# Idle products in the tensor engine's first waits, and q of units 6 to 10 transposed on the tensor engine

## The chip, the cores and the metric

The kernel runs on one core of a Trainium2 chip. The metric is the device time of one execution in microseconds. The engines are called as the profile calls them: PE multiplies matrices (PEld is its weight load), DVE and POOL work on vectors, ACT copies and activates, SP issues most transfers.

## The reference

A retention block and a feed-forward block without nonlinearity, in fp32:

```python
# q, k, v: (8, 8, 576, 64)   gamma[h] = 1 - 2**(-5 - h)
scores = 1/sqrt(64) * (q @ k.T)
ret = (scores * where(i >= j, gamma[h]**(i - j), 0)) @ v
x = ret.transpose(0, 2, 1, 3).reshape(4608, 512)
out = ((x @ w1) * (x @ w2) @ w3) @ w_out       # w1, w2: 512x1024, w3: 1024x1024, w_out: 1024x512
```

The four weight matrices arrive as 64-bit floats and are converted to fp32 on the chip.

## The kernel before

**Attention.** The eight batches go in four pairs, and the 576 positions in five pieces, one of 64 (the short one) and four of 128. A piece of a pair is a unit: unit g has pair g // 5 and piece g % 5, and there are 20. For a unit, `load` brings q, k and v with positions on the partitions (512 KB each, 256 KB for a short unit), in runs of 64 floats. `scale` multiplies q and v by the decays, mostly on POOL, in the first pair partly on ACT. `front` turns k and q so that the head's dimension lies on the partitions: PE transposes eight blocks of a tensor into two `tp` tiles of PSUM, and ACT copies these to `kT` and `qT`. `score` multiplies them and DVE masks (`pm`, line 246). `state` (line 265) sums k by v over the pieces, and ACT copies the sum to `sb`. `pv` (lines 293 and 300) makes the output, and ACT copies it to the feed-forward block's input `xT`.

**Loads by blocks.** `load_blocks` brings q or k in blocks of 32x32 instead, each in its transposed place: 16 transfers of 32 KB for a full unit, 8 for a short one, in runs of 32 floats. `scale_blocks` scales q in two halves on POOL, and `front_blocks` turns all blocks in place with one DVE transpose for each tensor (line 200), so that PE and ACT have no part in it. The units from 11 on have both q and k by blocks. In the kernel before, units 6 to 10 have q by blocks and k by `load` and `front`.

**Feed-forward.** `up` computes the products with w1 and w2 for 384 tokens and a quarter of the columns in seven products of halves (Strassen's scheme; lines 497, 502 and 523). Each of the seven is four fp32 matmuls of 128x128 by 192 columns. The first, p1, has no sums as operands; the second, S2 by T2, needs sums of weights (`strassen_weights`, `wS`, line 160) and of tokens (`strassen_tokens`, `T`, line 471). `down` does the rest with w3 @ w_out (line 603), which is multiplied out once (`w3_mm`, line 452).

**The order.** All engines work strictly in the order in which the program issues to them; the order is written out by hand at the end of the function. In the first 60 us loads of units 0 to 4, weight blocks (`load_block`, tiles `raw`) and their conversion on DVE and ACT (lines 370 to 402) alternate with the first units' attention and the first steps of `up`. SP issues the loads in that order. Weights are converted from five `raw` buffers. `convert(n)` puts n pieces of a conversion between other work on DVE.

After the weights, a loop runs over units 5 to 19. In its turn g it loads unit g + 2, turns unit g + 1 (`front`), does `down` or `up` steps from a list (`work`), then pv of g, state and scores of g + 1, and the scaling of q of unit g + 2.

**Memory in PSUM.** One pool, `acc`, of seven buffers in rotation, holds `tp`, `sc`, `xps`, `up`, `po` and the small `gps`. An eighth holds the state.

Of the kernel before, what the change touches and what calls it, by code (L numbers as in the profile page):

```python
# [8 lines left out]
F32 = mybir.dt.float32  # L9
# [31 lines left out]
def kernel(  # L41
# [13 lines left out]
    nc = tc.nc  # L55
# [6 lines left out]
    P = 128  # L62
# [6 lines left out]
    NC = (S + P - 1) // P  # L69
# [30 lines left out]
    acc = ctx.enter_context(tc.tile_pool(name="acc", bufs=7, space=PSUM))  # L100
# [33 lines left out]
    nc.scalar.dma_start(dq, decay_q)  # L134
    nc.scalar.dma_start(gk[:short, 0, :], decay_k[:short, :])
    nc.scalar.dma_start(gk[:, 1:, :], decay_k[short:, :].rearrange("(c p) h -> p c h", p=P))
    gps = acc.tile([P, NC, H], F32, tag="acc", name="gps")
    for c in range(NC):
        nc.tensor.transpose(gps[:sizes[c], c, :], dq[:, starts[c]:starts[c] + sizes[c]], ident[:H, :H])
    for c in (0, slice(1, NC)):  # L140
        n = short if c == 0 else P
        nc.vector.tensor_copy(gq[:n, c, :], gps[:n, c, :])

# [46 lines left out]
                out=part, in0=part, in1=gqs[:, :, n0:n0 + n].unsqueeze(3).to_broadcast([P, NP, n, BL]),  # L192
                op=ALU.mult)

    def front_blocks(g, names="kq"):
        c = g % NC
        n = sizes[c] // BL
        for nm in names:
            dst = pools["fr"].tile([P, 2, NP, P], F32, tag=nm + "T", name=nm + "T", bufs=1 if nm == "k" else 2)
            nc.vector.transpose(  # L200
                dst[:, :, :, :sizes[c]].rearrange("p b m (n x) -> p (b m) n x", x=BL),
                live["bl_" + nm, g][:, :, :n, :])
            live[nm + "T", g] = dst
# [13 lines left out]
    def front(g, names="kq"):  # L217
        c = g % NC
        sz = sizes[c]
        for nm in names:  # L220
            src = live[nm, g]
            dst = pools["fr"].tile([P, 2, NP, P], F32, tag=nm + "T", name=nm + "T",
                                   bufs=1 if nm == "k" and g >= NC else 2)
            for b in range(2):
                tp = acc.tile([P, NP, P], F32, tag="acc", name="tp")
                for p in range(NP):
                    h = b * H + 2 * p
                    nc.tensor.transpose(tp[:, p, :sz],  # L228
                                        src[:sz, h:h + 2, :].rearrange("p a d -> p (a d)"),
                                        ident[:sz, :sz])  # L230
                nc.scalar.copy(dst[:, b, :, :sz], tp[:, :, :sz])
            live[nm + "T", g] = dst
# [39 lines left out]
    def pv(g):  # L272
        i, c = divmod(g, NC)
        sz = sizes[c]
        live["x", g] = True
        qT, vs, pm = live["qT", g], live["v", g], live["pm", g]

        parts = []
        for n in range(NB):
            lo, hi = max(starts[c], n * TB), min(starts[c] + sz, (n + 1) * TB)  # L280
            if lo < hi:
                m = i * NB + n
                if ("xT", m) not in live:
                    live["xT", m] = xps[m % 4 == 3].tile([P, NP, 2, TB], F32, tag="xT", name="xT")
                parts.append((live["xT", m], lo - n * TB, lo - starts[c], hi - lo))

        banks = [acc.tile([P, 2, 2, P], F32, tag="acc", name="xps") for r in range(2)]
        order = [(b, n) for b in range(2) for n in range(2)]
        if c > 0:
            for m, (b, n) in enumerate(order):  # L290
                for r, j in ((0, 0), (0, 1), (1, 0), (1, 1)):
                    p = 2 * r + n
                    nc.tensor.matmul(banks[r][heads[j ^ r], b, n, :sz], live["sb", g][heads[j], b, p, :],  # L293
                                     qT[heads[j], b, p, :sz], start=(m == 0), stop=False,
                                     skip_group_check=True)
        for m, (b, n) in enumerate(order):
            for r in range(2):
                for half in range(2):
                    p, j = 2 * r + n, half ^ r
                    nc.tensor.matmul(banks[r][heads[half], b, n, :sz], vs[:sz, b * H + 2 * p + j, :],  # L300
                                     pm[:sz, b, j, p, :sz], start=(c == 0 and m == 0), stop=True,
                                     skip_group_check=True)
        for x, to, fr, n in parts:
            for r in range(2):
                nc.scalar.copy(  # L305
                    x[:, 2 * r:2 * r + 2, :, to:to + n].rearrange("p n b s -> p b n s"),
                    banks[r][:, :, :, fr:fr + n])
# [169 lines left out]
        minus(B[0][1], B[1][1], B[0][1])  # L477
        minus(T[2], B[1][0], T[1])

    def up(i, n, fp, conv=0, tail=True):  # L480
        m = every.index((i, n))
        while ("S", fp) not in live:
            assert go_on() is None
        if ("B", i, n) not in live:
            strassen_tokens(i, n)
        if fp == 0:
            live["ab", i, n] = (pools["ab3"] if m == 2 else ffn).tile([P, 2 * KF, TB], F32, tag="ab", name="ab")
        ab = live["ab", i, n]

        def product(ps, a, b):  # L490
            a, b = A(fp, a), live["B", i, n][b]
            new = ps is None
            if new:
                ps = acc.tile([P, 2, TB], F32, tag="acc", name="up")
            for w in range(2):
                for r in range(2):
                    nc.tensor.matmul(ps[:, w, :], a[:, w, r, :], b[:, r, :], start=(new and w == r == 0),  # L497
                                     stop=(w == r == 1), skip_group_check=True)
            return ps

        def plus(ps, to, sb):
            nc.vector.tensor_add(c[:, to], ps, c[:, sb])  # L502
            convert(conv)
            if aside:
                aside.pop(0)()


        c = ffn.tile([P, 4, 2, TB], F32, tag="c", name="c", bufs=1)
        p1 = product(None, "A11", "B11")
        nc.scalar.copy(c[:, 0], p1)  # L510
        plus(product(None, "S2", "T2"), 1, 0)
        plus(product(None, "S3", "T3"), 2, 1)
        p5 = product(None, "S1", "T1")
        plus(p5, 3, 2)
        plus(product(None, "A22", "-T4"), 2, 2)
        product(p1, "A12", "B21")
        nc.scalar.copy(c[:, 0], p1)  # L517
        product(p5, "S4", "B22")
        plus(p5, 1, 1)

        if fp == NQ - 1 and m + 1 < len(every) and has_x(*every[m + 1]) and ("B", *every[m + 1]) not in live:
            strassen_tokens(*every[m + 1])
        nc.vector.tensor_mul(ab[:, 4 * fp:4 * fp + 4, :], c[:, :, 0, :], c[:, :, 1, :])  # L523
        if tail:
            convert(conv)
# [130 lines left out]
    load(1, "v")  # L656
    load_block()
    scale(0, "q")
    front(0)
    convert(3)  # L660
    score(0)
    scale(0, "v")
# [6 lines left out]
    convert_up_to(2)  # L669
    load_block()  # L670
    scale(1, "q")
    front(1)
    convert(3)
    scale(1, "v")
    score(1)
# [4 lines left out]
    first_sums = strassen_weights(0)  # L680
    next(first_sums)
    pv(1)
    load(3, "kqv")
    load_block()
    strassen_tokens(0, 0, nc.vector)
# [1 line left out]
        pass  # L687
    scale(2, "q", True)
    aside.append(lambda: scale(2, "v", True))
    up(0, 0, 0, conv=2, tail=False)  # L690
    front(2)
    convert(1)
    scale(3, "q")
# [63 lines left out]
    carry(2, 2)  # L757
    weights_part.close()
    open_attention(ctx)
    load(NC, "kqv")  # L760
    load(NC + 1, "kv")
    load_blocks(NC + 1, "q")
    keep_stores.clear()
    store()
    todo = [(down, (0, 0), (0, 1)), (down, (1, 0), (1, 1)), (down, (0, 2), (1, 2))]
# [33 lines left out]
    front(NC)  # L799
    state(NC)  # L800
    score(NC)
    scale_blocks(NC + 1)
    in_blocks = [u > 2 * NC for u in range(G)] + [False] * 2
    for g in range(NC, G):
        c = g % NC
        n = -(-len(todo) // (NC - c))
        if g + 2 < G and not in_blocks[g + 2]:
            load(g + 2, "k")
            load_blocks(g + 2, "q")
        if g + 1 < G:  # L810
            scale(g + 1, "v")
            if not in_blocks[g + 1]:
                front(g + 1, "k")
                front_blocks(g + 1, "q")
        half = (n + 1) // 2
        if in_blocks[g + 1]:
            scale_blocks(g + 1)
            work(1)
            front_blocks(g + 1)
            half = max(half - 1, 0)  # L820
        if in_blocks[g + 2]:
            load_blocks(g + 2, "q")
            load_blocks(g + 2, "k")
        work(half)
        pv(g)

        if g + 2 < G:
            queue = nc.scalar if in_blocks[g + 2] else nc.sync
            load(g + 2, "v", queue)
            if in_blocks[g + 2] and (g + 2) % NC != NC - 1:  # L830
                load(g + 2, "k", queue)
        if g + 1 < G:
            state(g + 1)
            score(g + 1)
        if g + 2 < G and not in_blocks[g + 2]:
            scale_blocks(g + 2)
        if g == NC + 1:
            strassen_tokens(1, 0)
            todo.extend((up, 1, 0, fp) for fp in range(2))
        work(n // 2)  # L840
        if c == NC - 1:
            add_pair(g // NC)
# [44 lines left out]
```

## Time and profile before

| | |
|---|---|
| median of 3 runs | 864.8 us (864.07 to 865.4) |
| profiled execution | 864.07 us |
| its span, first to last instruction | 862.4 us |
| busy: PE, PEld | 840.2 us (97%), 764.8 us (89%) |
| busy: DVE, ACT, POOL | 473.8 us (55%), 181.6 us (21%), 115.3 us (13%) |
| chain that ended last: PE, DVE, DMA | 85%, 7%, 4% |
| transfers | 63.21 MB, mean 73 GB/s; some 200 GB/s up to 70 us |

An engine's share is an average over stages with different limits. A group's idle time is that of the engine ahead of its instructions; its releaser is inferred from semaphore events. A matmul in fp32 is two records in the trace.

### The profile page before, as it was taken

Reading aid. Unit: us, or ns where it says so; the run is one execution under the profiler, and the core shown is the slowest. Engines: PE = TensorE matmul, PEld = TensorE weight load, DVE = VectorE, ACT = ScalarE, POOL = GpSimd, SP = SyncE. Lnnn points to the kernel's source line nnn. Section 1 sums busy time; section 2 is a strip of 40 time slices with the busy share of each in tenths; the row PEclk is TensorE's granted clock in tenths of the full one; section 3 lists DMA queues with packets and bytes.
Section 4 is the critical chain, followed back from the end, with each engine's and each line's share of the span. In section 5 each row is a group of like instructions: output and inputs, shape, how many; then the busy total and the mean of one; then the engine's idle time right before and its main releaser. Section 6 shows DMA issues by size and latency. Waiting matters only on the chain.

```text
span 862.4 us, 15290 instructions
## 1 busy us (share of the span) xinstructions
PE 840.2 (97%) x6269; PEld 764.8 (89%) x6269; DVE 473.8 (55%) x794; ACT 181.6 (21%) x364; POOL 115.3 (13%) x96
## 2 busy tenths in 40 slices
PE   5899999999999999999999999999999999999998
PEld 5789999644888999999999999999999999999996
DVE  4889998986655344543544453535543434335343
ACT  3666333343121211101111101101101100001000
POOL 3000020001313223203023030230300101000000
PEclk9999999999999999999999999999999999999999
DMA  9994453444346534515142426061300000000001
GB/s 191 218 215 126 99 98 99 122 135 75 48 86 140 110 53 80 87 36 112 32 86 33 77 50 102 22 120 24 52 25 26 2 25 1 25 25 1 25 1 49
DMA packets 204918, 63.21 MB, mean 73 GB/s; under 512 B 186920, under 2 KB 195112, under 8 KB 204848
## 3 DMA queue, kind: packets, MB, share of 16 engines
q1 hardware_dynamic: 172208, 54.07, 30.3%
q10 hardware_dynamic: 32640, 8.16, 5.2%
q8 instruction: 49, 0.80, 0.4%
q14 instruction: 21, 0.17, 0.1%
HBM read 52.76 MB, written 9.44 MB: 72 GB/s over the span
## 4 chain that ended last, share of the span: by engine, by line
PE 85%; DVE 7%; DMA 4%; issue 2%; ACT 1%; SPq 1%; POOL 0%; DVEq 0%; ACTq 0%; POOLq 0%
PE up L497 46%; PE po L603 24%; PE ps L452 4%; PE sc L243 4%; PE xps L300 3%; PE xps L293 2%; PE st L265 1%; DVE c L502 1%; DMA ld_q<-in_q_dram 1%; PE tp L228 1%; DMA raw<-in_moe_w_dram 1%; DVE e L391 1%; DMA ld_k<-in_k_dram 1%; DVE w L402 1%; SPq L725 0%
## 5 line engine op out<-in xcount | busy, mean ns | idle before, releaser
L502 DVE TENSOR_TENSOR c<-up,c 128x384 f32<-128x384 f32 x240 | 133.2, 555 | 183.8 <-PE up L497 179.0
L497 PE MATMUL up<-xT,wA 128*128 128x192 f32 x1152 | 212.1, 327 | 0.7 <-ACT xT L305 0.7
L497 PEld LDWEIGHTS up<-xT,wA 128*128 128x128 f32 x1152 | 190.7, 190 | 3.5 <-ACT xT L305 1.0
L497 PE MATMUL up<-T,wS 128*128 128x192 f32 x768 | 140.6, 326 | 2.4 <-DVE T L471 2.1
L497 PEld LDWEIGHTS up<-T,wS 128*128 128x128 f32 x768 | 127.3, 190 | 2.9 <-issue 2.9
L603 PE MATMUL po<-w3o,ab 128*128 128x256 f32 x456 | 104.3, 380 | 0.3 <-ACT ot L625 0.3
L603 PEld LDWEIGHTS po<-w3o,ab 128*128 128x128 f32 x456 | 85.8, 190 | 12.5 <-ACT ot L625 0.7
L607 DVE TENSOR_TENSOR ot<-po,ot 128x256 f32<-128x256 f32 x90 | 38.2, 424 | 75.0 <-PE po L603 72.2
L497 PE MATMUL up<-xT,wS 128*128 128x192 f32 x384 | 70.6, 327 | 0.6 <-DVE c L502 0.5
L517 ACT COPY c<-up 128x384 f32<-128x384 f32 x48 | 22.9, 477 | 226.2 <-PE up L497 222.0
L246 DVE TENSOR_TENSOR pm<-sc,mask 128x512 f32<-128x512 f32 (+1 forms) x80 | 45.5, 629 | 45.3 <-PE sc L243 45.2
L497 PE MATMUL up<-T,wA 128*128 128x192 f32 x384 | 70.2, 326 | 0.0
L603 PE MATMUL po<-wB,forms 128*128 128x256 f32 x288 | 65.2, 379 | 0.4 <-DVE forms L573 0.4
L497 PEld LDWEIGHTS up<-xT,wS 128*128 128x128 f32 x384 | 63.6, 190 | 1.5 <-DVE c L502 1.5
L497 PEld LDWEIGHTS up<-T,wA 128*128 128x128 f32 x384 | 63.7, 190 | 0.0
L603 PEld LDWEIGHTS po<-wB,forms 128*128 128x128 f32 x288 | 54.6, 190 | 8.2 <-PE po L603 0.8
L214 POOL TENSOR_TENSOR ld_v<-ld_v,gk 128x1024 f32<-128x1024 f32 (+1 forms) x17 | 33.0, 1942 | 199.9 <-DMA ld_v<-in_v_dram 149.8
L452 PE MATMUL ps<-wo,w3T 128*128 128x512 f32 x128 | 56.1, 596 | 2.9 <-DVE w3T L406 2.9
L452 PEld LDWEIGHTS ps<-wo,w3T 128*128 128x128 f32 x128 | 23.8, 190 | 34.5 <-issue 30.6
L471 POOL TENSOR_TENSOR T<-xT,T 128x384 f32<-128x384 f32 x20 | 20.9, 1044 | 216.1 <-PE up L497 214.5
L523 DVE TENSOR_TENSOR ab<-c 128x768 f32<-128x768 f32 x48 | 47.3, 986 | 3.8
L510 ACT COPY c<-up 128x384 f32<-128x384 f32 x48 | 22.8, 476 | 117.8 <-PE up L497 69.1
(73 smaller groups left out, 796.2 us busy)
## 6 DMA issues: line engine op xcount, KB each, us to landing
raw<-in_moe_w_dram SPq DMA_DIRECT2D x64, 128.0 KB, 3.0
bl_q<-in_q_dram SPq DMA_DIRECT2D x208, 32.0 KB, 2.1
out_dram<-ot SPq DMA_DIRECT2D x24, 256.0 KB, 2.0
bl_k<-in_k_dram SPq DMA_DIRECT2D x136, 32.0 KB, 2.2
raw<-in_moe_w_dram SPq DMA_DIRECT2D x8, 512.0 KB, 7.7
raw<-in_moe_w_dram SPq DMA_DIRECT2D x16, 256.0 KB, 7.5
ld_k<-in_k_dram SPq DMA_DIRECT2D x8, 512.0 KB, 6.9
ld_v<-in_v_dram SPq DMA_DIRECT2D x8, 512.0 KB, 7.0
```

What stands on the lines that cost most here:

```text
L214: nc.gpsimd.tensor_tensor(out=t, in0=t, in1=gam[:sz, c].unsqueeze(1).unsqueeze(3).to_broadcast([sz, 2, H, D]), op=ALU.mult)
L243: nc.tensor.matmul(sc[j][:sz, p, :sz], kT[hs, b, p, :sz], qT[hs, b, p, :sz], start=True, stop=True)
L246: nc.vector.tensor_mul(pm[:sz, b, j, :, :sz], sc[j][:sz, :, :sz], mask[:sz, :sz].unsqueeze(1).to_broadcast([sz, NP, sz]))
L300: nc.tensor.matmul(banks[r][heads[half], b, n, :sz], vs[:sz, b * H + 2 * p + j, :], pm[:sz, b, j, p, :sz], start=(c == 0 and m == 0), stop ...
L452: nc.tensor.matmul(ps, live["w3T", ft][:, g, :], live["wo"][:, g, :], start=(g == 0), stop=(g == KF - 1))
L497: nc.tensor.matmul(ps[:, w, :], a[:, w, r, :], b[:, r, :], start=(new and w == r == 0), stop=(w == r == 1), skip_group_check=True)
L502: nc.vector.tensor_add(c[:, to], ps, c[:, sb])
L510: nc.scalar.copy(c[:, 0], p1)
L517: nc.scalar.copy(c[:, 0], p1)
L523: nc.vector.tensor_mul(ab[:, 4 * fp:4 * fp + 4, :], c[:, :, 0, :], c[:, :, 1, :])
L603: nc.tensor.matmul(ps[nm], a[A][:, f, :], live["W"][B][:, f, :], start=(f == 0 and not on), stop=(f == NP - 1), skip_group_check=True)
L607: nc.vector.tensor_add(ot[:, to[0], to[1]], ps[nm], ot[:, sb[0], sb[1]])
```

## The change

The new kernel issues products of the 128x128 identity by itself into an `acc` tile that nobody reads: ten before the transposes of the decays (`gps`), four between k and q of unit 0, six between k and q of unit 1, four behind pv of unit 1, and eight in the first `up`, behind p1. For units 6 to 10, q comes by `load`, is scaled by `scale` and turned by `front` on PE and ACT; `load_blocks`, `scale_blocks` and `front_blocks` remain for units 11 to 19.

```diff
+    warm = acc.tile([P, P], F32, tag="acc", name="idle")
+    for _ in range(10):
+        nc.tensor.matmul(warm, ident, ident, start=True, stop=True)
     gps = acc.tile([P, NC, H], F32, tag="acc", name="gps")
...
+    def keep_busy(n):
+        t = acc.tile([P, P], F32, tag="acc", name="idle")
+        for _ in range(n):
+            nc.tensor.matmul(t, ident, ident, start=True, stop=True)
...
-    def up(i, n, fp, conv=0, tail=True):
+    def up(i, n, fp, conv=0, tail=True, busy=0):
...
         nc.scalar.copy(c[:, 0], p1)
+        if busy:
+            keep_busy(busy)
         plus(product(None, "S2", "T2"), 1, 0)
...
-    front(0)
+    front(0, "k")
+    keep_busy(4)
+    front(0, "q")
...
-    front(1)
+    front(1, "k")
+    keep_busy(6)
+    front(1, "q")
...
     pv(1)
+    keep_busy(4)
     load(3, "kqv")
...
-    up(0, 0, 0, conv=2, tail=False)
+    up(0, 0, 0, conv=2, tail=False, busy=8)
...
-    load(NC, "kqv")
-    load(NC + 1, "kv")
-    load_blocks(NC + 1, "q")
+    for g in (NC, NC + 1):
+        load(g, "kqv")
...
-    scale_blocks(NC + 1)
+    scale(NC + 1, "q")
...
-            load(g + 2, "k")
-            load_blocks(g + 2, "q")
+            load(g + 2, "kq")
...
-                front(g + 1, "k")
-                front_blocks(g + 1, "q")
+                front(g + 1)
...
-            scale_blocks(g + 2)
+            scale(g + 2, "q")
```

More of the change, by code (lines that the diff above doesn't have):

```diff
@@ L193, in scale_blocks, with front_blocks @@
                 op=ALU.mult)
-    def front_blocks(g, names="kq"):
+    def front_blocks(g):
         c = g % NC
         n = sizes[c] // BL
-        for nm in names:
+        for nm in "kq":
             dst = pools["fr"].tile([P, 2, NP, P], F32, tag=nm + "T", name=nm + "T", bufs=1 if nm == "k" else 2)
```

## The prediction

> **What bounds the kernel now.** I read the page first, then the windows by stage, then what PE waited for, then PE's timeline, and last the DMA queue and the chain that ended last. The page:
>
> ```profile
> PE 840.2 (97%) x6269; PEld 764.8 (89%) x6269; DVE 473.8 (55%) x794; ACT 181.6 (21%) x364; POOL 115.3 (13%) x96
> ```
>
> PE is busy for 840.2 of 862.4 us. The windows say where the missing 22 us are not (length, then busy time of PE, PEld, DVE, ACT and POOL, then granted clock, DMA share, GB/s):
>
> ```profile
> 57.60:110.00 52.40, 52.40 (x436) 50.95 (x437) 49.62 (x92) 25.04 (x53) 0.00 (x0) 1.00 0.51 119
> 232.00:328.00 96.00, 95.60 (x1011) 86.64 (x1010) 44.72 (x74) 19.09 (x42) 20.19 (x17) 1.00 0.45 91
> ```
>
> Between 57.6 and 110 us PE has no idle time at all, and in the 96 us in which units 5 to 10 are prepared it has 0.40 us. There an instruction added to PE moves the end by its full length, and one taken from DVE (44.72 of 96) moves nothing. What PE waited for in the first 75 us (total, times, longest):
>
> ```profile
> PE gps L139 <- DMA dq<-decay_q_dram: 6.2, 1, 6.2
> PE tp L228 <- POOL ld_q L214: 3.0, 3, 1.7
> PE up L497 <- DVE T L471: 2.1, 1, 2.1
> PE tp L228 <- DMA ld_k<-in_k_dram: 1.2, 1, 1.2
> ```
>
> With the smaller ones these are 14.0 us, all before 57.55. The first 58 us are thus the only place where the products that are read by nobody can win or lose. PE's timeline (start, length, operation, idle time before it and its releaser):
>
> ```profile
> 16.00 1.97 PE L228 MATMUL tp<-ident,ld_k 128*128 128x128 f32 x8
> 19.63 1.97 PE L228 MATMUL tp<-ident,ld_q 128*128 128x128 f32 x8 [1.67 <-POOL ld_q L214]
> 24.67 1.15 PE L265 MATMUL st<-ld_v,ld_k 128*64 128x64 f32 x32 [0.50 <-POOL ld_v L214]
> 33.15 1.54 PE L497 MATMUL up<-T,wS 128*128 128x192 f32 x8 [2.08 <-DVE T L471]
> 41.26 1.04 PE L228 MATMUL tp<-ident,ld_k 128*128 128x128 f32 x8
> 42.13 1.04 PE L228 MATMUL tp<-ident,ld_q 128*128 128x128 f32 x8
> 44.42 1.06 PE L228 MATMUL tp<-ident,ld_k 128*128 128x128 f32 x8 [1.25 <-DMA ld_k<-in_k_dram]
> 48.81 1.09 PE L228 MATMUL tp<-ident,ld_q 128*128 128x128 f32 x8 [0.26 <-POOL ld_q L214]
> 57.55 1.54 PE L497 MATMUL up<-T,wS 128*128 128x192 f32 x8 [0.30 <-DVE wS L160]
> ```
>
> Two things are to be seen. The same eight transposes take 1.97 us at 16 and 19.6 us and 1.04 us at 41 us: PE runs at half speed early on, though the clock column of the windows reads 1.00 there. And PE comes late to nothing after the first step: it stands still for 1.25 us at 44.42, 0.26 at 48.81 and 0.30 at 57.55, waiting for a load, for a load that POOL scales, and for a weight. Whether those three can come earlier is told by the DMA queue over the first 75 us (packets, MB, share of 16 engines)
>
> ```profile
> q1 hardware_dynamic: 31040, 14.68, 98.9%
> ```
>
> and by the chain that ended last (start, length):
>
> ```profile
> 7.27 9.96 DMA ld_q<-in_q_dram
> ...
> 43.88 9.16 DMA raw<-in_moe_w_dram
> ...
> 53.14 0.43 DVE e L370
> ```
>
> The queue is full (98.9%) until about 71 us. SP's timeline shows each issue following the one before it, with long ones (ld_q from 34.43 for 7.05 us) where the queue has no room. Unit 3's q lands at 46.70 and POOL scales it from 46.86 to 48.76; the raw block issued at 43.88 lands at 53.04, and the seven DVE operations that need it or stand behind it end at 57.41, just before PE's 57.55.
>
> **The change, part by part.** First, the idle products. An fp32 product shows as two records (one `product` of four matmuls is x8). A record of 128 columns takes 0.109 us at full speed: 0.87 us for eight from the start at 41.26 to that at 42.13. In the early rows it takes 1.97/1.04 = 1.9 times that, 0.21. The 10 before `gps` are 20 records, 4.3 us at the slow rate; `ident` is done at 1.37 us, so they end near 5.7, before `gps` at 6.25, which waits for a load in any case. The 4 between k and q of unit 0 are 0.87 us (1.7 slow) against a wait of 1.11. The 6 in unit 1 are 1.31 us (2.6 slow) against 1.67. The 4 behind pv(1) are 0.87 against 0.74, so p1 starts 0.13 late. The 8 behind p1 are 1.74 against 2.08.
>
> What they win: at full speed the rows before 24 us shrink. Beside like rows later on, unit 0's k and q give 0.4 each, its scores 0.9, state 0.9, pv 0.8, unit 1's k and q 0.9 each, its scores 0.6: 5.8 us. But unit 1's q starts when POOL has scaled it (17.36 to 19.58, after the landing at 17.23), so all before that turns into a longer wait at 19.63. The 1.5 us from q and scores of unit 1 turn into a longer wait at 24.67, where `st` needs v, landed at 22.64 and scaled by 24.61. PE then does st, pv and xT as before. DVE gets its scores up to 1.5 us earlier, so T is ready near 31.6 instead of 33.1, but PE is in its fillers to about 33.0 (29.6 + 1.57 + 1.74). The first step starts 0.1 to 0.2 us earlier, and the wait for ld_k at 44.42 takes that back.
>
> What they cost, if the clock stays low and all fillers run slow: q of unit 1 about 1.3 us late, the first step 0.9 to 1.2 late, and the waits at 44.42 and 48.81 have 1.51 to give. From both sides the sum at 57.55 is 0; as bounds I keep -0.3 (the wait there gone) and +0.5 (an overrun somewhat above my 1.2). Each `idle` takes one of seven `acc` buffers; in order of allocation none meets one still being read (the nearest: the second k tile of unit 2 takes p1's, copied by ACT at 40.16, written at 41.7).
>
> A page of the Trainium skill would have this part worth more: "TensorE: Matmul & The Clock Gate", Part 1 and the closing table, says that the array starts at half clock and that some 3.4 us of sustained work release it, so that PE should be kept busy through waits. The halved rows agree with that; yet its advice as a gain would put all 5.8 us into the total, and the landings at 17.23, 22.64, 44.28 and 46.70 let none of it through. By the page's rule alone the sum would be near 863.
>
> Second, q of units 6 to 10 as one plain load each. Gone: 72 block issues on SP (four times 16, once 8; 16 of them took 10 us of SP's time), five transposes on DVE (four of 1.23 us, a shorter one) and ten half-tile scalings on POOL. Added: five loads, five whole-tile scalings on POOL (1.9 to 2.6 us by its rows of L214), ten copies on ACT (0.58 each, ACT busy 19.09 of 96) and forty transposes on PE. Only PE's count. They stand directly behind k's, as at 41.26, so a full unit's q adds 0.87 us, four of them 3.48. Unit 10 is the short one:
>
> ```profile
> 239.79 0.71 PE L228 MATMUL tp<-ident,ld_k 64*128 64x64 f32 x8
> 240.34 0.66 PE L228 MATMUL tp<-ident,ld_q 64*128 64x64 f32 x8
> ```
>
> From start to start 0.55. The sum is 3.48 + 0.55 = +4.03 us. From below 3.85 (107 and 53 ns a record, back to back); from above 4.65, if each eight costs the 1.02 that k's take in the chain by themselves.
>
> The part adds a wait: q's transposes need POOL's scaling, and behind them on PE stands everything else. Before, only DVE waited for it. Let the loads start when SP got to the first block, and give them a plain load's 7 us. Unit 6: landed by about 220, scaled by 223, needed at 243.9. Unit 7: issued at 242.6, scaled by 253, needed at 261. Unit 8: issued at 261.6, scaled by 271, needed at 280. Unit 9: 278.1, 288, 299. Unit 10: 299.0, 307, 314. The smallest margin is 7 us, so this wait costs nothing; without that cover each microsecond of lateness would be one on the end. The two more `acc` tiles per unit meet score tiles that DVE has read (the scores' pm starts at 259.39, the last tile of q would be written near 261.6): 0, at most 0.3 a unit. Nothing later gives the 4 us back: from 330 us to the end PE waits 0.5 us in all, and behind its own products.
>
> The profiled execution took 864.07 us, 1.7 beside its span of 862.4. It becomes 864.07 + 0 + 4.03 = 868.1; the median of the runs is 0.7 above it (864.8), so 868.8.
>
> **The rivals.** Not slower: the first step's earlier start pulls the transfers with it. The place is SP between 27 and 47 us, where raw blocks reuse buffers that DVE has converted; the waits view puts 1.7 us of the issue at 43.88 down to a DVE conversion. If DVE's order and not the queue's room set it, the raw block and ld_q of unit 3 could land earlier by as much as PE gains, at most the 5.8 us: 868.8 - 5.8 = 863.0. It decides from 4.0 us of gain on. Against it: the block that it overwrites was converted at 30.41, 13 us before, and the 0.1 to 0.2 us of head start is all there is to pull.
>
> Slower than forecast: PE waits at the new transposes, for POOL or for an `acc` buffer, by 0.5 us in each of five units: 871.3. Against it stand the margins above.
>
> Slower at the start: the fillers overrun by more than the 1.51 us of slack, say by 1 us: 869.8. That needs the clock to stay low after 24 us, where the profile has it high.
>
> If the unread products were dropped from the program, the time would be the forecast's, since I price them at 0.
>
> **How the numbers follow.** The forecast has 0.83, with 867.6 to 869.9 as its own range (864.07 + 3.85 - 0.3, and 864.8 + 4.65 + 0.5). The waits at the transposes have 0.07, the overrun 0.05, the transfers pulled forward 0.05. A difference of 0.2%, 1.7 us, is about what a measurement of this kernel can tell from none (its three runs lie 1.3 apart). The range goes to 867.5 and 870.3: below little more than that, above for part of the two slower cases. Faster: 0.03, from the pulled transfers at full size; same: 0.04, from these at partial size and from scatter; slower: 0.93.
>
> **What would show it.** Each eight transposes of unit 1 take about 1.05; PE's waits before 19.63 and 24.67 grow; the wait before unit 3's k stays at 44.4, and the second `up` starts its second product near 57.55 as before. From 239.8 on, five rows tp<-ident,ld_q follow those of k with no wait, and each unit's pv comes later by 0.87 more than the last, to 4.0 at 328 us; L200 has five instructions fewer for qT. The forecast is wrong if 57.55 moves by more than half a microsecond, or if a wait for POOL stands before a tp of units 6 to 10.

## The result and the profile after

The changed kernel takes 869.82 us in the median of six runs (868.95 to 870.43), the kernel before beside it 865.12 (864.07 to 865.51): a ratio of 1.0055, with a 95% interval of 1.0042 to 1.0068. That is 4.7 us more; 4.0 were forecast. The profiled execution has a span of 867.7 us, 5.3 more than before.

The page's first part, and the same two stretches of the windows:

```profile
PE 849.2 (98%) x6373; PEld 774.4 (89%) x6373; DVE 468.4 (54%) x789; ACT 186.0 (21%) x374; POOL 113.7 (13%) x91
```

```profile
57.60:110.00 52.40, 52.40 (x439) 51.18 (x438) 49.64 (x92) 25.41 (x53) 0.00 (x0) 1.00 0.53 118
232.00:328.00 96.00, 96.00 (x933) 87.52 (x935) 37.33 (x65) 22.50 (x50) 19.13 (x12) 1.00 0.43 88
```

PE is still without idle time in both, and does its old work later in the second; DVE gave up 7.4 us of the 96, for which nobody waited. PE's waits in the whole span, the longest ones:

```profile
PE ps L461 <- DVE w3T L415: 2.9, 3, 1.3
PE tp L237 <- DMA ld_k<-in_k_dram: 2.2, 2, 1.6
PE tp L237 <- POOL ld_q L223: 2.2, 3, 1.6
PE st L274 <- POOL ld_v L223: 1.8, 2, 1.1
PE po L614 <- DVE ab L580: 1.7, 1, 1.7
```

The first was there before. The second to fourth are the waits of the first 50 us, in new places. The last is new. It stands in the first `down`, for an operand that DVE makes: `ab` is the product of the two `up` results, `forms` are sums of it. PE's timeline shows the places (start, length, operation, idle time and releaser):

```profile
14.96 1.91 PE L237 MATMUL tp<-ident,ld_k 128*128 128x128 f32 x8 [0.59 <-DMA ld_k<-in_k_dram]
16.66 2.35 PE L151 MATMUL idle<-ident 128*128 128x128 f32 x12
20.57 1.10 PE L237 MATMUL tp<-ident,ld_q 128*128 128x128 f32 x8 [1.56 <-POOL ld_q L223]
...
32.94 1.54 PE L506 MATMUL up<-T,wS 128*128 128x192 f32 x8
...
44.59 1.06 PE L237 MATMUL tp<-ident,ld_k 128*128 128x128 f32 x8 [1.63 <-DMA ld_k<-in_k_dram]
48.91 1.09 PE L237 MATMUL tp<-ident,ld_q 128*128 128x128 f32 x8 [0.18 <-POOL ld_q L223]
57.35 1.46 PE L506 MATMUL up<-T,wS 128*128 128x192 f32 x8
```

The first step's second product starts at 32.94 instead of 33.15, unit 3's k waits 1.63 us for its load instead of 1.25, and the second step's second product is 0.20 us ahead of before. Further on, first in the kernel before:

```profile
226.82 5.50 PE L603 MATMUL po<-w3o,ab 128*128 128x256 f32 x24
232.72 3.69 PE L603 MATMUL po<-wB,forms 128*128 128x256 f32 x16 [0.40 <-DVE forms L573]
...
313.63 1.57 PE L497 MATMUL up<-xT,wA 128*128 128x192 f32 x8
```

and then in the kernel after:

```profile
226.54 1.89 PE L614 MATMUL po<-w3o,ab 128*128 128x256 f32 x8
230.18 3.72 PE L614 MATMUL po<-w3o,ab 128*128 128x256 f32 x16 [1.74 <-DVE ab L580]
233.73 3.62 PE L614 MATMUL po<-wB,forms 128*128 128x256 f32 x16
...
262.01 1.09 PE L237 MATMUL tp<-ident,ld_k 128*128 128x128 f32 x8
262.94 1.04 PE L237 MATMUL tp<-ident,ld_q 128*128 128x128 f32 x8
263.81 5.34 PE L614 MATMUL po<-w3o,ab 128*128 128x256 f32 x24
...
317.99 0.66 PE L237 MATMUL tp<-ident,ld_q 64*128 64x64 f32 x8
318.57 1.57 PE L506 MATMUL up<-xT,wA 128*128 128x192 f32 x8
```

The first down starts 0.28 us ahead of before (226.54 against 226.82), then stands for 1.74. From there each full unit's q takes 0.87 us (262.94 to 263.81) without a wait. Against before, PE is 1.01 us late at the forms' product (233.73 against 232.72) and 4.94 at the step behind unit 10's transposes (318.57 against 313.63), so the five units cost 3.93; the remaining 0.4 of the 5.3 come in small pieces later.

### The profile page after: what moved, and what is told of

Same layout as the page of the kernel before. It is cut to its first block, busy times and chain, and to the rows that moved or that the text cites. A ratio compares the mean times of both kernels' runs of the same rounds, so it can differ in the third digit from the quotient of the medians.

```text
span 867.7 us, 15391 instructions
## 1 busy us (share of the span) xinstructions
PE 849.2 (98%) x6373; PEld 774.4 (89%) x6373; DVE 468.4 (54%) x789; ACT 186.0 (21%) x374; POOL 113.7 (13%) x91
## 4 chain that ended last, share of the span: by engine, by line
PE 84%; DVE 6%; issue 2%; ACT 1%; DMA 1%; SPq 0%; DVEq 0%; ACTq 0%
PE up L506 44%; PE po L614 24%; PE ps L461 4%; PE sc L252 4%; PE xps L309 3%; PE xps L302 2%; DVE c L511 2%; PE tp L237 1%; PE st L274 1%; DVE e L400 1%; DVE w L411 1%; DVE m L386 0%; DVE w3T L415 0%; DMA raw<-in_moe_w_out_dram 0%; ACT e L389 0%
```

## The experiments

All times are medians; each ratio is against runs of the kernel before on the same chip, whose median lay between 864.02 and 864.43 us. My first theory after the comparison was that three parts add up: idle products, transposes, and a collision of POOL with DVE near 222 us.

**Each part alone.** First only the idle products on the kernel before:

```diff
+    for _ in range(10):
+        nc.tensor.matmul(warm, ident, ident, start=True, stop=True)
     gps = acc.tile([P, NC, H], F32, tag="acc", name="gps")
...
-    front(0)
+    front(0, "k")
+    keep_busy(4)
+    front(0, "q")
...
-    front(1)
+    front(1, "k")
+    keep_busy(6)
+    front(1, "q")
...
     pv(1)
+    keep_busy(4)
...
-    up(0, 0, 0, conv=2, tail=False)
+    up(0, 0, 0, conv=2, tail=False, busy=8)
```

> The kernel before with the idle products alone. Theory (the three parts add: idle products, q's transposes, and a collision of POOL and DVE near 222 us): 0.5 us less than before, 864.6 against 865.1, since the second product of the second up starts near 57.35 instead of 57.55 and PE is 0.5 us ahead at 67 us; the wait before the forms near 230 us stays at 0.4. Rival (the idle products cost, by their overrun or by shifting what runs against what later): 0.5 to 1.4 us more than before, with a wait of over 1 us near 230 us.

862.5 us against 864.4, ratio 0.9979 (0.9970 to 0.9989): a gain of 1.9 us, where the theory had 0.5 and the rival a loss. The loads of units 6 to 10 are those of before. In its profile PE is 0.31 us ahead at the second step's second product, and the wait before the forms is gone.

Then only the other part, without the idle products:

```diff
-    load(NC, "kqv")
-    load(NC + 1, "kv")
-    load_blocks(NC + 1, "q")
+    for g in (NC, NC + 1):
+        load(g, "kqv")
...
-    scale_blocks(NC + 1)
+    scale(NC + 1, "q")
...
-            load(g + 2, "k")
-            load_blocks(g + 2, "q")
+            load(g + 2, "kq")
...
-                front(g + 1, "k")
-                front_blocks(g + 1, "q")
+                front(g + 1)
...
-            scale_blocks(g + 2)
+            scale(g + 2, "q")
```

> The kernel before with plain loads, POOL scalings and PE transposes for q of units 6 to 10, and no idle products. Theory: 4.0 us of transposes and 1.3 to 1.5 us of wait near 230 us, 5.3 to 5.5 us more than before, 870.5. Rival (the collision came from the idle products' shift): 4.0 us more, 869.1, and a wait of 0.4 us near 230 us.

868.45, ratio 1.0045 (1.0031 to 1.0059), 4.0 us more, the rival's number. The wait in the first down is there, but 0.50 us long. So the collision has another size in the two kernels' traces, and the parts do not simply add.

**The collision.** DVE in the kernel after, around the sums of w3 (line 551), and POOL beside it:

```profile
220.56 1.22 DVE L551 TENSOR_TENSOR w3o<-w3o 128x1024 f32<-128x1024 f32 x1
...
222.16 2.46 DVE L551 TENSOR_TENSOR wB<-w3o 128x1024 f32<-128x1024 f32 x1
...
225.01 2.45 DVE L551 TENSOR_TENSOR wB<-w3o,wB 128x1024 f32<-128x1024 f32 x1
...
227.85 1.21 DVE L551 TENSOR_TENSOR wB<-w3o,wB 128x1024 f32<-128x1024 f32 x1
```

```profile
221.22 2.32 POOL L223 TENSOR_TENSOR ld_q<-ld_q,gq 128x1024 f32<-128x1024 f32 x1 [3.68 <-DMA ld_q<-in_q_dram]
223.50 2.88 POOL L223 TENSOR_TENSOR ld_v<-ld_v,gk 128x1024 f32<-128x1024 f32 x1
```

The two sums that begin while POOL scales unit 6 take twice as long; the one that had begun before POOL, and the one behind, do not. The rows also show that "twice" is chance, and that the engines take turns. The second sum ends at 224.62, 1.08 us behind the end of POOL's q (223.54), and the third at 227.46, 1.08 behind that of its v (226.38): each ends as if it had begun when POOL's row ended, 0.14 us short of its usual 1.22. POOL in turn needs 2.32 instead of its usual 1.90 us for q, because the first sum runs until 221.78. A shorter operation shows the same in the kernel before. It begins while POOL's row runs and takes 2.27 us; in the kernel after, where POOL is done by then, it takes 0.69:

```profile
229.41 2.61 POOL L214 TENSOR_TENSOR ld_v<-ld_v,gk 128x1024 f32<-128x1024 f32 x1
230.30 2.27 DVE L573 TENSOR_TENSOR forms<-ab 128x512 f32<-128x512 f32 x1
```

POOL's row ends at 232.02 and DVE's at 232.57, 0.55 later.

To tell POOL from the loads that land in these microseconds, POOL is held back and the loads are left. In the kernel after, q and v of unit 6 are multiplied by a copy of the decays (`late`, taken where `after` is set) that ACT writes only behind the first `down`:

```diff
+    late = const.tile([P, 2, H], F32, tag="late", name="late")
...
     down((2, 0), (2, 1), ((0, 0), (0, 1)))
+    nc.scalar.copy(late[:, 0, :], gq[:, 1, :])
+    nc.scalar.copy(late[:, 1, :], gk[:, 1, :])
...
-    scale(NC + 1, "q")
+    scale(NC + 1, "q", after=True)
...
-            scale(g + 1, "v")
+            scale(g + 1, "v", after=g == NC)
```

> The kernel after, in which POOL scales q and v of unit 6 by a copy of the decays that ACT makes behind the first down, so near 236 us instead of 221 to 226; the loads stay where they are. Theory (POOL's scaling doubles DVE's sums of w3): the four sums take 1.22 us each, the wait of 1.74 us near 230 us is gone or below 0.3, and the time is 1.4 to 1.7 us less than after, 868.3. Rival (the loads that land in these microseconds slow DVE): two of the sums stay at 2.4 us, the wait stays, and so does the time, 869.8.

867.21, ratio 1.0031 (1.0020 to 1.0042). Its DVE and POOL:

```profile
220.06 1.22 DVE L555 TENSOR_TENSOR w3o<-w3o 128x1024 f32<-128x1024 f32 x1
...
221.66 1.22 DVE L555 TENSOR_TENSOR wB<-w3o 128x1024 f32<-128x1024 f32 x1
...
223.26 1.22 DVE L555 TENSOR_TENSOR wB<-w3o,wB 128x1024 f32<-128x1024 f32 x1
```

```profile
234.00 1.90 POOL L227 TENSOR_TENSOR ld_q<-ld_q,late 128x1024 f32<-128x1024 f32 x1 [16.80 <-ACT late L777]
```

All sums take 1.22 us, PE waits for nothing over 0.1 us from 200 to 330 us, and the difference of the two ratios to before (1.0053 for after in later runs, below) is 1.9 us. The loads of q and v land at 220.54 and 222.65, among the sums as before (221.06 and 223.11 in the kernel after). So it is POOL's work, not the landing, that holds DVE up. The other way to take the collision out is unit 6 by blocks again, with units 7 to 10 as in the kernel after:

```diff
-    def front_blocks(g):
+    def front_blocks(g, names="kq"):
...
-        for nm in "kq":
+        for nm in names:
...
-    for g in (NC, NC + 1):
-        load(g, "kqv")
+    load(NC, "kqv")
+    load(NC + 1, "kv")
+    load_blocks(NC + 1, "q")
...
-    scale(NC + 1, "q")
+    scale_blocks(NC + 1)
...
-                front(g + 1)
+                front(g + 1, "k")
+                front(g + 1, "q") if g > NC else front_blocks(g + 1, "q")
```

> The kernel after with q of unit 6 by blocks again, scaled in halves on POOL and turned by DVE; units 7 to 10 as after. Theory: one full unit's transposes less (0.87 us) and POOL's scalings of unit 6 back near 226 us, where they cost 0.4 us of wait: 2.2 us less than after, 867.6, and PE's delay against before grows by 0.87 a unit from unit 7 on. Rival (the transposes of every unit cost more than 0.87 us, and there is no collision to take away): 0.9 to 1.1 us less than after.

866.13, ratio 1.0019 (1.0010 to 1.0028), about 3 us less than after, more than either theory had: 0.87 of transposes and the whole wait of 1.74 went, none of 0.4 came. POOL's scaling begins at 226.78 here, 0.87 us behind the start of the first down; in the kernel before it begins 0.73 ahead of that start. In its trace units 7 to 9 each have 0.9 us from k's to q's end, as expected.

**What the idle products win by.** In the traces the 16 KB transfers of queue q8, kind instruction, fall at other times with them (41.2 and 51.5 us instead of 47.6 and 54.5). The next two kernels try whether that is the gain:

```diff
+    for _ in range(32):    # 64 in the second
+        nc.tensor.matmul(warm[:1, :1], ident[:1, :1], ident[:1, :1], start=True, stop=True)
     gps = acc.tile([P, NC, H], F32, tag="acc", name="gps")
```

> The kernel before with 32 unread products of one element each, all ahead of the transposes of the decays: as many PE instructions as the 32 idle products, but no work in any later wait. Theory (the idle products' gain of 1.9 us comes from PE's program being 128 instructions longer early on, so that its code comes in at other moments and no longer delays one of 16 parts of the weight block that the second up waits for): a code transfer near 41 us and none near 47.6, that block landed by 50.3 to 51.8 instead of 53.0, the second product of the second up at 56.3 to 57.4, and 862.5 to 863.2, about as with the idle products. Rival (they win by filling waits and by a clock that rises sooner): nothing is filled, so 864.4, like before, and 57.5 to 57.6 for that product.

> The same with 64 such products, 256 PE instructions of 64 bytes, one whole code transfer of 16 KB. Theory (code transfers): they fall where they fell before (near 28, 47.6 and 54 us), the weight block lands near 53 again, and the time is that of before, 864.4. Rival 1 (any early PE work wins, by the clock): as with 32 or more, 862.5. Rival 2 (it costs its length): 864.4 plus up to 1.

864.57 with 32 (ratio 1.0008, 0.9999 to 1.0017) and 864.56 with 64 (1.0005, 0.9996 to 1.0014). The transfers did move with 32, to 42.8 and 52.4 us, and the weight block landed at 51.61, and it won nothing: this theory falls. More PE instructions ahead of the decays' transposes are not enough. The next pair splits the 32 products on the kernel before into the last 12 (the first diff) and the first 20 (the second):

```diff
     pv(1)
+    keep_busy(4)
...
-    up(0, 0, 0, conv=2, tail=False)
+    up(0, 0, 0, conv=2, tail=False, busy=8)
```

```diff
+    for _ in range(10):
+        nc.tensor.matmul(warm, ident, ident, start=True, stop=True)
     gps = acc.tile([P, NC, H], F32, tag="acc", name="gps")
...
-    front(0)
+    front(0, "k")
+    keep_busy(4)
+    front(0, "q")
...
-    front(1)
+    front(1, "k")
+    keep_busy(6)
+    front(1, "q")
```

> The kernel before with only the last 12 idle products: 4 behind pv(1) and 8 behind p1. Theory (the gain sits at the first step: without them PE stands still for most of 28.7 to 33.1 us, and in part of the executions the granted clock falls to half for 3.4 us inside the first step, which is then up to 1.7 us late and pushes DVE's conversions beside POOL's scaling): the whole gain, 862.5 against 864.2, clock 1.00 from 29 to 39 us, the second product of the second up at 56.3 to 57.6. Rival (the early clock matters, since all before 20 us is faster with it): 864.2.

> The kernel before with only the first 20 idle products: 10 ahead of the decays' transposes, 4 in unit 0, 6 in unit 1. Theory (the gain sits at the first step): at most 0.5 us of gain, 863.7 to 864.5, and a low clock possible in 29 to 39 us. Rival (early clock): 862.5.

The last 12 alone: 863.32, ratio 0.9990 (0.9981 to 0.9998), 0.7 us gained or somewhat more. The first 20 alone: 862.47, ratio 0.9982 (0.9973 to 0.9991), 1.6 us, nearly the whole. So the theory of the first step does not give the whole gain. The windows of the second kernel (clock behind the five busy times) show the very drop that I had made responsible, in an execution of 862.92 us, 0.45 above the median:

```profile
29.00:33.00 4.00, 1.66 (x9) 1.39 (x10) 3.79 (x7) 3.43 (x11) 0.00 (x0) 1.00 0.96 235
33.00:36.00 3.00, 3.00 (x13) 2.73 (x14) 3.00 (x7) 2.71 (x10) 0.00 (x0) 0.72 1.02 216
36.00:39.00 3.00, 3.00 (x15) 3.00 (x14) 1.61 (x5) 1.27 (x3) 0.00 (x0) 0.72 1.07 262
```

The last kernel of this group has idle products only ahead of the decays' transposes:

```diff
+    for _ in range(6):
+        nc.tensor.matmul(warm, ident, ident, start=True, stop=True)
     gps = acc.tile([P, NC, H], F32, tag="acc", name="gps")
```

> The kernel before with six full idle products ahead of the decays' transposes and none elsewhere; the order of unit 5's and 6's loads behind the last weight blocks comes out as in the kernels with ten (SP waits for the last conversion and not for the one before it, 1.1 us later against PE). Theory (the idle products' gain has two parts: the wait of 0.40 us before the forms goes, since POOL's scaling of unit 6 begins behind the sums that matter, and some 0.5 to 1 us come from the first units being done sooner): the first part and little of the second, 863.2 to 863.7 against 864.0, no wait near 232 us. Rival 1 (all of the gain comes from that order of loads): 862.4. Rival 2 (none of it): 864.0 and a wait of 0.4 near 232 us.

864.58, ratio 1.0009 (0.9999 to 1.0020), and the wait at the forms is there (0.40 us): rival 2, nothing. SP's loads do come in the expected order, so that order alone does not bring the gain. Ahead of the decays' transposes six products win nothing, and products in units 0 and 1 (with ten ahead) win 1.6.

Two comparisons across these kernels say more of where the gain lies. First, the traces. From the start of the first down to the product with the forms PE takes 5.18 us in every kernel with products in units 0 and 1 and q of unit 6 by blocks, and 5.90 to 6.34 in the five without such products (before, 32 and 64 of one element, the last 12, the six). From there to the end all those with q by blocks in units 6 to 10, and k as before, agree within 0.2 us. In the first group POOL's scaling of unit 6 begins 0.87 us or more behind the first down's start (or is held back); in the second it begins between 1.01 ahead and 0.56 behind. So 0.7 to 1.2 us of the traces' difference lie where POOL and DVE meet. That is one trace of each kernel, and why POOL falls later with the early products is open.

Second, the clock. Of the 21 runs of the kernel before beside the last 12 and the first 20, twelve have a mean granted clock of 0.998, which 3.4 us at half clock would give, and nine 1.00; their times are 864.93 and 863.39 us in the mean. In the three other sets of its runs the two groups lie 1.2, 0.8 and 1.9 us apart. With the last 12 no run reads 0.998, and their median of 863.32 is about the time of the nine. So the 0.7 us of the last 12 go with a low clock that no longer comes; that it causes them is not shown, because the trace of the kernel before is of a run at 1.00. The first 20, at 862.47, are 0.9 us better than even the nine, with one run at 0.998 among them.

**Toward a better kernel.** The kernel before with all 32 idle products, and unit 6's scalings held back in the same way, q still by blocks:

```diff
+    nc.scalar.copy(late_b, gqs[:, :, 2:2 + P // BL])
+    nc.scalar.copy(late[:, 1, :], gk[:, 1, :])
...
-    scale_blocks(NC + 1)
+    scale_blocks(NC + 1, after=True)
...
-            scale(g + 1, "v")
+            scale(g + 1, "v", after=g == NC)
```

> The kernel before with the idle products, and with POOL's scalings of unit 6 (q by blocks, and v) held back by copies of the decays that ACT makes behind the first down. Theory (POOL doubles what DVE does beside it): the sums behind the first down take 0.69 to 0.95 us each, no wait for the forms near 231 us, as there was none of note with the idle products alone; so 0 to 0.4 us less than those, 862.1 to 862.5. Rival (the scaling comes too late for the transposes on DVE): a wait at the scores of unit 6, 1 us more.

862.76, ratio 0.9987 (0.9978 to 0.9996): no better than the idle products alone, which had no wait left there. DVE's operations do keep their length (0.68 to 0.95 us), but nobody was waiting for them.

On top of that, units 9 and 10 with their k by blocks too, so that PE is spared its transposes:

```diff
-    in_blocks = [u > 2 * NC for u in range(G)] + [False] * 2
+    in_blocks = [u > 2 * NC - 2 for u in range(G)] + [False] * 2
```

> The same, and units 9 and 10 have k by blocks too, so that PE turns neither: the change's second part the other way round. Theory (PE is the bound there and each eight transposes cost their length): 0.93 and 0.5 us less, 1.4 in all, 860.9. Rival (SP's issues, 32 for unit 9 at 0.55 us, or DVE's transposes come too late for the scores): a wait of PE before the scores of unit 9 or 10 that takes 1.4 us or more back.

873.14, ratio 1.0104 (1.0089 to 1.0120): the rival's side, and far beyond its price. PE's waits between 290 and 360 us, in a trace of the shortest of its five runs (870.29):

```profile
PE up L512 <- DVE c L517: 6.1, 1, 6.1
PE sc L258 <- DVE qT L211: 1.2, 1, 1.2
```

The transposes that PE is spared come too late from SP's blocks and DVE, and what DVE waits for holds up the steps behind.

Last, the kernel after, unchanged (no edit, hence no diff), on the chip that ran the last 12 and the first 20:

> The kernel after once more, beside the others on one chip. Theory (parts add): idle products -1.9, transposes +3.95, POOL beside DVE's sums of w3 +1.3 to +1.7, so 867.6 to 868.0 against 864.2 for before. Rival (the parts do not add; the idle products' gain is lost in this kernel): 869.0 or more.

868.9, ratio 1.0053 (1.0040 to 1.0065): 4.9 us over before, the rival's figure within 0.1 us. By the ratios (1.0053 and 1.0055 against 0.9979) it is 6.4 to 6.6 us over the idle products alone: 3.93 of transposes, 1.74 of the wait, and 0.7 to 0.9 more. Some 0.5 of these the traces show: the way from the first down to the forms is 2.0 us longer (7.19 against 5.18), and that from the forms to the end 4.2. The rest is less than the intervals are wide. The version that beats both kernels is thus the one with the idle products and without the other part: 862.5, and with the first 20 alone 862.47.

## Why the prediction was right, and where it was not

**The transposes held.** 4.03 us were forecast from 4 x 0.87 + 0.55, and 3.93 are in the trace, with 0.49 for the short unit. That PE would not wait at them for POOL or for a buffer held too: unit 10's q, the tightest, was scaled by 309.6 and used at 317.99.

**The idle products were put at 0 from both sides, and they win 1.9 us.** Of the chain of steps a part came out as drawn: unit 1's q fell to 1.10 us, the wait at 24.66 grew, the first step came 0.2 earlier, and the wait at 44.59 took that in. Unit 1's k did not fall (1.91 us, at a granted clock of 0.50), and its q started at 20.57 instead of 19.63, because POOL scaled it from 18.61 and not from 17.36. What failed is the bound of -0.3. It was read from one execution and ended at 57.55, and the gain is not bounded there: part of it lies at the first down, and part goes with executions unlike the one that I read. The kernels without products in units 0 and 1 spread widely (862.5 to 866.2 with six ahead, 863.4 to 865.9 with 32 of one element), while with the first 20 all eleven runs lie between 861.8 and 863.2: the early products seem to remove the longest executions. One kernel speaks against that: the one with the 32 and unit 6 held back, in which two of eleven runs lie at 864.5 and 865.9. Code transfers are excluded as the cause, and the first step's own fillers (the last 12) as the main one; a low clock can stand for a part, as above. How the rest comes about is open. The advice of the Trainium skill's page "TensorE: Matmul & The Clock Gate" (Part 1 and the closing table) to keep PE busy, which I priced at nothing, has the right sign here; the 5.8 us that I had worked out for it are three times the 1.9 measured, and that the clock brings them is not shown.

The windows of the kernel after also show that the products do not hold the clock: a low stretch comes back with them,

```profile
14.00:16.00 2.00, 1.41 (x19) 1.30 (x14) 1.88 (x4) 1.94 (x5) 0.00 (x0) 0.75 1.37 225
16.00:18.00 2.00, 2.00 (x12) 2.00 (x11) 0.86 (x2) 1.17 (x2) 0.00 (x0) 0.50 1.07 301
18.00:20.00 2.00, 1.01 (x7) 0.81 (x6) 0.07 (x1) 0.00 (x0) 1.39 (x1) 0.90 1.28 238
```

and the six of unit 1 took 2.35 us, near my slow figure of 2.6, not 1.31.

**"Only PE's count" was wrong by 1.3 us.** I asked of POOL's scaling of unit 6 only whether it comes too late, and found 20 us to spare; it came too early. With the loads in blocks it began at 226.09, during the last of the four sums of w3, and held up the operations behind them, of which PE felt 0.40 us. With plain loads it began at 221.22, on top of two of the sums, and PE felt 1.74. Where the scaling falls is a matter of a microsecond or two: in the kernel with plain loads and no idle products it began at 218.75, hit one sum, and cost 0.50. There SP issues unit 5's first load earlier (206.47, against 207.67 in after): in that kernel and in before the longest wait ahead of this load ends with one conversion of the weights, and in after with the next one (DVE `e` done at 206.8 in before, the next at 207.6 in after).

**The sum was near by luck.** A gain of 1.9 that I did not have and a loss of 1.3 to 1.7 that I did not have nearly cancel. The two rivals on the slow side did not come true as drawn: the wait appeared ahead of the new transposes, not at them. The rival on the fast side did not come true either: SP's issue that decides it was at 44.07 in after, 43.88 before.

## What to carry to other kernels

Where PE has no idle time, an added PE instruction costs its length; here the sum of such lengths came within 0.1 us of the trace. When work on POOL is moved earlier, look at what DVE does at the new moment, not only at who waits for the result. What a change does to the start of a kernel, where everything waits for transfers, cannot be bounded from one execution: look at the spread of the runs first, and at whether it goes with their granted clock.

## What was not expected of the hardware

A DVE sum or product of SBUF tiles that began while POOL scaled did not run beside it at a lower speed: it ended about its own length after POOL's row. In thirteen of the traces 174 such operations took over 1.1 times their shortest length, and 173 of them ended that length, less 0.12 to 0.15 us, behind the end of POOL's row. In this way sums over 128x1024 took 2.45 us instead of 1.22, and forms over 128x512 2.27 instead of 0.69; with the scaling moved away all took 1.22. The 672 DVE operations with an operand in PSUM that began beside POOL (`c<-up,c`, `pm<-sc,mask`, `ot<-po,ot`) kept their length within a tenth. The granted clock fell to 0.50 from about 15 to 18.5 us in after, although from 6.39 us on PE had waited for at most 1.09 us at a time, and in other executions in the middle of the first step (0.72 on average from 33 to 39 us). 32 more products of one element in PE's program moved a 16 KB transfer of kind instruction by some 5 us (47.6 to 42.8), without a change of the time that can be told from none (ratio 1.0008, 0.9999 to 1.0017).
